# Another fixed order for the tasks of an attention stage

## The chip, the cores and the metric

The kernel runs on one core of a Trainium2 chip. The metric is the device time of one execution in microseconds (us), the median of three runs. The core's engines are named as in the profile: PE is TensorE (matmuls and transposes), PEld its loading of weights, DVE is VectorE, ACT is ScalarE, POOL is GpSimd and SP is SyncE, which here only starts DMA transfers.

## The reference

An attention over B = 4 batches, H = 8 heads, S = 576 positions and D = 64, with a second, linear "memory" branch, and behind it a mixture of 8 experts over all N = 2304 tokens, of which each token takes one:

```
scores = where(causal, -1e9, q @ k.T / sqrt(D))
a      = exp(scores - rowmax);  a /= a.sum(-1) + 1e-9
local  = a @ v
q_p    = elu(q) + 1
mem    = (q_p @ M_prev) / (q_p . z_prev + 1e-6)
x      = g * mem + (1 - g) * local          # g = sigmoid(beta) per head
# x as [2304, 512]
e      = argmax(x @ w_gate);  gate_w = softmax(x @ w_gate)[e]
eom    = sigmoid(x @ w_output_gate)[e]
out    = gate_w * eom * (relu(x @ w1[e]) @ w2[e])   # D = 512, F = 1024
```

All data are float32.

## The kernel before

**Tasks.** The attention, the routing and the first steps of the expert stage are cut into 1,181 small tasks. A task has a name, an engine and a function that issues a few instructions. The heads are taken two by two: a pair g (0 to 15) holds two heads of batch g // 4, and its 576 query positions are five tiles q (0 to 3 of 128 rows, 4 of 64). The names, with b for a batch:

- SSg_q: the scores of a query tile, on TensorE. One matmul is written as three with high and low parts (hi, lo). For q of 1 to 3 the two heads stand in the two halves of 64 rows of the array (L570); SSg_1 also holds q = 0. SSg_4 uses the full array (L557).
- Mg_q_j: mask and maximum on VectorE (L628, L596), from PSUM to the tile st. Eg_q_j: exponential and row sum on ScalarE. Tg_q_j: transposes of the probabilities on TensorE into a PSUM tile pt (L645, L614). Vg_q_j: the copy from pt to PT (L492).
- Pg_r_i: the product of probabilities and values, for query rows from r on (0 or 256; for the last pair 0, 128, ... 512). A matmul writes 64 columns of the array's output (L680). Og_r: its copy to oT (L492).
- Cg, Rg, F0g, F1g, F2g: the split of a pair's data into hi and lo, and phi, the elu + 1; F2 is on VectorE (L520).
- MEb_q: the memory product of a batch's query tile, 2 x 4 small matmuls over halves of 64 rows (L736), into two tiles me_0 and me_1. N1b_q and N2b_q normalise and scale it on VectorE (L742, L749), Gb_q sums logits (L752).
- PVb_q: transposes of oT on TensorE (L799); Wb the weights 1 / sum (L767, L768) and Yb_q the weighting on VectorE (L803); XD and OUT add and store.
- LTb_i: local logits, four matmuls side by side of 32 columns each (L828), LC their copy, LS their transposes, LY, LB, LA, RT, Tgate, Tpos, RK, GP, GS the routing. PLlq_h, YLlq_h, XLlq_h are what the last batch has for PV, Y and XD.
- Z...: first steps of the expert with the most tokens, called the star. The expert stage behind the attention starts with its product he (L1123).

**Modes.** Each task of TensorE has a mode, by the shape of its tile of the array: F (full array: SSg_4, transposes, PV, PL, RK, GP), R (row tiles: the other scores and ME), C (column tiles: P) and L (narrow column tiles: LT).

**What sets the order.** No scheduler decides: a string `ORDER` lists all tasks, and a loop issues them in that order. So the string sets the program order of every engine. Behind a colon stands the engine of a copy (tasks V, O, C and LC), ACT or DVE, since either can do it:

```
    def copy(e, dst, src):
        (A.copy if e == "ACT" else V.tensor_copy)(dst(), src())
...
    by = {t.name: t for t in jobs}
    for item in ORDER:
        name, _, eng = item.partition(":")
        by[name].fn(eng)
```

Engines run on their own and wait for each other by semaphores. Every TensorE task writes PSUM tiles from pools that give out free buffers: tag s (scores) has 4 buffers, tag pt (transposed probabilities) 2, and tag m has 2, for everything else: P, ME (which takes both), PV, LT, LS, RK, GP. A task waits until the readers of a buffer's former tile are done.

Of the kernel before, what the change touches and what calls it, by code (L numbers as in the profile page):

```python
# [55 lines left out]
C3:DVE F12 P1_0_0 E2_1_0 V1_4_1:DVE T2_0 load4 E1_3_0 E1_3_1 V2_0:DVE SS2_2 R3 M2_2_0 M2_2_1 O0_256:ACT O1_0:ACT SS2_3 T2_1 T1_3_1 load_v3 E2_2_0
V2_1:ACT M2_3_0 V1_3_1:ACT TS1_0 E2_3_0 SS2_4 T1_3_0 V1_3_0:ACT M2_3_1 MW1 F13 F04 E2_2_1 T2_2_0 T2_3_0 TS1_1 ranks M2_4_0 P1_256_0 C4:DVE E2_3_1 F22 MC1
V2_2_0:ACT SS3_1 M3_0_0 V2_3_0:ACT P1_256_1 T2_2_1 M3_1_0 M2_4_1 E2_4 V2_2_1:ACT E3_0_0 load5 F23 O1_256:DVE M3_0_1 T2_3_1 TS2_0 load6 E3_0_1 E3_1_0
V2_3_1:DVE SS3_2 ME0_0 M3_2_1 T2_4 E3_2_1 R4 M3_1_1 wgz V2_4_0:ACT N10_0 N20_0 V2_4_1:ACT F06 SS3_4 T3_2_1 T3_0 M3_2_0 ME0_1 F14 V3_0:ACT M3_4_0
V3_2_1:ACT SS4_1 M3_4_1 E3_2_0 N10_1 SS4_2 E3_1_1 N20_1 T3_1 T3_2_0 C5:ACT P2_0_0 P2_256_0 TS2_1 E3_4 M4_0_0 V3_1:ACT M4_0_1 F24 M4_2_1 G0_1 M4_2_0  # L60
V3_2_0:ACT O2_0:ACT E4_0_1 E4_0_0 T3_4 M4_1_1 E4_1_1 E4_2_1 P2_256_1 V3_4_0:DVE TS3_0 M4_1_0 O2_256:DVE T4_0 SS3_3 E4_1_0 load_v4 E4_2_0 V3_4_1:DVE
M3_3_0 ME0_4 C6:ACT V4_0:ACT T4_2_0 SS4_4 V4_2_0:ACT R5 N10_4 T4_2_1 R6 TS3_1 N20_4 M3_3_1 M4_4_0 V4_2_1:ACT T4_1 E3_3_0 M4_4_1 load7 E3_3_1 V4_1:ACT
ME0_3 SS4_3 E4_4 T3_3_1 V3_3_1:ACT T3_3_0 N10_3 V3_3_0:ACT N20_3 M4_3_0 F16 E4_3_0 M4_3_1 ME0_2 N10_2 TS4_0 F05 SS5_1 SS5_2 N20_2 F26 T4_4 M5_0_0
M5_0_1 E4_3_1 P3_0_0 V4_4_0:DVE P3_256_0 O3_0:ACT E5_0_0 load9 P4_0_0 E5_0_1 M5_1_0 G0_3 P3_256_1 load_v5 F15 C7:ACT M5_2_0 W0 O3_256:ACT T4_3_0
O4_0:ACT F07 V4_4_1:DVE F25 E5_1_0 R7 T4_3_1 PV0_2 M5_2_1 M5_1_1 PV0_1 SS5_4 V4_3_1:ACT E5_1_1 E5_2_1 V4_3_0:DVE T5_0 Y0_2 G0_4 V5_0:ACT E5_2_0 Y0_1
M5_4_0 SS5_3 G0_0 M5_4_1 LT0_0 load8 XD0_1 LC0_0:DVE T5_2_0 V5_2_0:ACT XD0_2 M5_3_1 T5_1 PV0_4 E5_4 M5_3_0 T5_2_1 SS6_2 SS6_1 V5_2_1:DVE F09 V5_1:ACT
E5_3_0 E5_3_1 Y0_4 OUT0_2 M6_0_0 LT0_1 F08 M6_2_1 LC0_1:ACT T5_4 load_v7 OUT0_1 E6_0_0 V5_4_0:ACT F19 M6_2_0 LM2 LS0 SS6_4 TS5_1 V5_4_1:ACT TS5_0
E6_2_1 F17 M6_1_0 TS4_1 T5_3_1 T5_3_0 LY0 XD0_4 M6_0_1 E6_0_1 LB0 G0_2 V5_3_1:ACT V5_3_0:ACT PV0_0 P4_256_0 M6_1_1 T6_2_1 F18 LA0 RT0_0 Y0_0 E6_1_1
E6_1_0 RT0_1 T6_0 SS7_1 XD0_0 P4_256_1 P5_256_0 O4_256:ACT V6_0:ACT V6_2_1:DVE M6_4_0 RT0_2 E6_2_0 C8:ACT R8 F27 RT0_3 RT0_4 M7_0_0 P5_0_0 P5_256_1
OUT0_4 T6_1 CA0 F28 E7_0_0 O5_0:ACT M6_4_1 E6_4 O5_256:DVE T6_2_0 load_v6 V6_2_0:ACT M7_0_1 M7_1_1 ME1_0 SS6_3 M7_1_0 SS7_3 load_v8 V6_1:ACT load10  # L70
E7_1_1 RX0 N11_0 E7_0_1 C9:ACT T6_4 N21_0 V6_4_0:ACT E7_1_0 PV0_3 M6_3_1 E6_3_1 M6_3_0 P6_0_0 Y0_3 V6_4_1:DVE TS6_0 E6_3_0 T7_0 O6_0:DVE M7_3_0 M7_3_1
# [4 lines left out]
SS9_1 O6_256:ACT E8_3_1 F013 O7_0:DVE T8_2_1 T8_1 F210 V8_2_1:ACT F211 M9_0_0 M9_0_1 PV1_0 T8_2_0 E8_3_0 V8_1:ACT P7_256_0 Tgate40 M9_1_1 W1 E9_0_1
V8_2_0:ACT Y1_0 M9_1_0 XD1_0 P7_256_1 load12 E9_0_0 T8_3_0 O7_256:ACT G1_4 G1_3 E9_1_1 V8_3_0:ACT PV1_1 OUT1_0 E9_1_0 F113 CJ0 LM3 load_v9 PV1_2
T8_3_1 Y1_1 Y1_2 SS8_4 M8_4_0 T9_0 M8_4_1 PV1_3 LT1_0 C11:ACT V8_3_1:ACT XD1_1 SS9_3 SS9_2 E8_4 V9_0:ACT G1_2 Y1_3 OUT1_1 M9_3_1 M9_3_0 load_v10 R11
LT1_1 XD1_2 T9_1 V9_1:ACT E9_3_0 SS9_4 LC1_0:DVE LC1_1:DVE LS1 TS8_0 XD1_3 M9_2_1 T8_4 E9_3_1 M9_2_0 LY1 V8_4_0:ACT SS10_1 LB1 OUT1_3 RK0 Tpos10
V8_4_1:ACT OUT1_2 T9_3_1 E9_2_1 PV1_4 LA1 M10_0_0 T9_3_0 Y1_4 RT1_0 V9_3_1:ACT M10_0_1 T9_2_1 E9_2_0 RT1_1 Tpos20 M9_4_0 V9_2_1:ACT C12:ACT P8_256_0  # L80
P8_0_0 Tpos30 M10_1_1 M10_1_0 P8_256_1 Tpos40 M9_4_1 RT1_2 CB0 F213 E10_0_1 V9_3_0:ACT T9_2_0 E10_0_0 E10_1_0 V9_2_0:ACT O8_0:DVE T10_0 E9_4 RT1_3
E10_1_1 V10_0:ACT O8_256:DVE RT1_4 SS10_2 M10_2_1 M10_2_0 E10_2_1 SS10_3 TS9_1 ME2_0 M10_3_0 R12 N12_0 load_v11 RX1 T10_1 SS10_4 SEL0_3 V10_1:ACT
E10_3_0 SEL0_2 ZI T9_4 N22_0 V9_4_0:ACT G2_0 TS9_0 E10_2_0 ME2_3 M10_3_1 SS11_1 C13:ACT V9_4_1:DVE E10_3_1 N12_3 R13 XD1_4 T10_2_1 T10_3_0 N22_3
V10_3_0:DVE M10_4_0 M11_0_0 E11_0_0 V10_2_1:ACT P9_256_0 P9_0_0 P9_256_1 M11_1_0 O9_0:ACT TS8_1 G2_3 T10_2_0 load15 O9_256:ACT T10_3_1 OUT1_4 F015
M10_4_1 V10_2_0:ACT M11_0_1 V10_3_1:ACT M11_1_1 Tgate11 Tgate31 E11_1_0 E10_4 E11_0_1 E11_1_1 SEL0_1 ME2_1 N12_1 SS11_3 N22_1 SS11_4 T10_4 RK1
V10_4_0:ACT MW3 T11_0 M11_4_0 Tpos11 M11_3_0 load14 TS10_1 V10_4_1:ACT V11_0:ACT MC3 T11_1 M11_3_1 V11_1:ACT ME2_4 Tpos21 CA1 CJ1 CB1 SS11_2 M11_4_1
E11_4 SS12_1 E11_3_1 N12_4 N22_4 T11_4 ZC M11_2_1 E11_3_0 TS11_1 M11_2_0 Z1 Z2 Tpos31 load_v12 M12_0_0 Z3 Z4 G2_1 V11_4_0:DVE Z5 P11_0_0 TS11_0
O11_0:ACT P10_256_0 P10_0_0 P10_256_1 F115 Tpos41 Z6 Z7 E12_0_0 Tgate21 M12_0_1 Z8 Z9 Z10 V11_4_1:DVE O10_0:ACT O10_256:DVE TS10_0 T11_3_0 T11_3_1
V11_3_1:DVE E11_2_1 M12_1_0 M12_1_1 ZN ME2_2 E12_0_1 C14:ACT N12_2 V11_3_0:ACT Tgate41 N22_2 E11_2_0 SS12_3 W2 T11_2_1 V11_2_1:ACT T11_2_0 SEL1_3
SS12_4 E12_1_0 PV2_1 T12_0 load_v14 V11_2_0:ACT E12_1_1 V12_0:ACT M12_3_1 M12_3_0 F215 P11_256_0 G2_2 SEL1_4 M12_4_0 Y2_1 E12_3_1 E12_3_0 SS13_1  # L90
P11_256_1 M12_4_1 SEL1_2 T12_1 M13_0_0 T12_3_1 M13_1_0 O11_256:ACT M13_0_1 V12_1:ACT M13_1_1 E12_4 XD2_1 PV2_4 PV2_3 R14 Y2_4 E13_1_1 T12_3_0 E13_0_1
SS12_2 SS13_3 XD2_4 OUT2_1 OUT2_4 V12_3_1:ACT V12_3_0:DVE M12_2_1 G2_4 E13_1_0 GA1 E13_0_0 T12_4 Y2_3 V12_4_0:ACT E12_2_1 F014 LT2_0 M12_2_0 LT2_1
T13_0 F012 SEL1_1 XD2_3 V12_4_1:DVE T13_1 LC2_0:DVE LC2_1:ACT V13_0:DVE M13_3_0 LS2 E12_2_0 V13_1:ACT SS13_2 T12_2_0 T12_2_1 E13_3_0 V12_2_1:ACT LY2
P12_0_0 M13_3_1 TS12_0 SEL0_4 load_v13 V12_2_0:ACT M13_2_0 O12_0:ACT PV2_0 LB2 M13_2_1 E13_2_0 SS13_4 T13_3_0 PV2_2 Y2_0 F112 F114 T13_2_0 Y2_2
V13_2_0:DVE XD2_0 Tgate50 Tgate51 OUT2_3 M13_4_0 E13_2_1 E13_3_1 F212 V13_3_0:ACT F214 P12_256_0 P13_0_0 P12_256_1 C15:DVE R15 O13_0:ACT SS14_1
# [1708 lines left out]
```

## Time and profile before

| what | value |
|---|---|
| median of 3 runs | 468.71 us (468.43 to 469.22) |
| profiled execution | 468.34 us |
| its span, first to last instruction | 466.3 us |
| TensorE busy | 456.7 us, 98% |
| VectorE busy | 284.9 us, 61% |
| ScalarE busy | 262.4 us, 56% |
| GpSimd busy | 271.1 us, 58% |
| granted TensorE clock, mean over the span | 0.996 of full speed |
| attention, up to the start of the expert stage's product he | 201.81 us |

Shares are means over the whole span. Busy time of TensorE counts from a matmul's start to its modelled end, and matmuls overlap, so it is an upper bound; starts are exact. The profiled execution is one; its time lies 0.37 us below the median.

### The profile page before, as it was taken

Reading aid. Unit: us, or ns where it says so; the run is one execution under the profiler, and the core shown is the slowest. Engines: PE = TensorE matmul, PEld = TensorE weight load, DVE = VectorE, ACT = ScalarE, POOL = GpSimd, SP = SyncE. Lnnn points to the kernel's source line nnn. Section 1 sums busy time; section 2 is a strip of 40 time slices with the busy share of each in tenths; the row PEclk is TensorE's granted clock in tenths of the full one; section 3 lists DMA queues with packets and bytes.
Section 4 is the critical chain, followed back from the end, with each engine's and each line's share of the span. In section 5 each row is a group of like instructions: output and inputs, shape, how many; then the busy total and the mean of one; then the engine's idle time right before and its main releaser. Section 6 shows DMA issues by size and latency. Waiting matters only on the chain.

```text
span 466.3 us, 10798 instructions
## 1 busy us (share of the span) xinstructions
PE 456.7 (98%) x3517; PEld 354.8 (76%) x3517; DVE 284.9 (61%) x851; ACT 262.4 (56%) x625; POOL 271.1 (58%) x274
## 2 busy tenths in 40 slices
...
GB/s 239 204 144 143 21 216 158 158 58 199 30 153 30 86 181 99 59 142 153 47 265 324 299 309 170 328 46 346 265 202 341 115 208 221 124 147 182 29 31 39
DMA packets 30119, 75.90 MB, mean 163 GB/s; under 512 B 4307, under 2 KB 4839, under 8 KB 30058
## 3 DMA queue, kind: packets, MB, share of 16 engines
...
q14 instruction: 28, 0.23, 0.1%
...
## 4 chain that ended last, share of the span: by engine, by line
PE 88%; DVE 3%; issue 2%; POOL 2%; ACT 2%; DVEq 1%; POOLq 0%; ACTq 0%
PE py L1432 18%; PE h L1432 17%; PE po L680 10%; PE pt L645 8%; PE s L570 7%; PE me L736 4%; PE hp L1458 3%; PE cy L1601 3%; PE ch L1601 3%; PE sd L557 3%; PE pt L614 2%; PE px L1400 2%; PE he L1123 1%; PE pv L799 1%; PE pl L904 1%
## 5 line engine op out<-in xcount | busy, mean ns | idle before, releaser
L633 ACT ACTIVATE st<-st,nm 128x128 f32<-128x128 f32 (+3 forms) x128 | 71.4, 562 | 3.7 <-DVE nm L628 3.6
L1465 POOL TENSOR_TENSOR hl<-hT,hh 128x512 fp32r<-128x512 f32 x32 | 43.5, 1380 | 40.6 <-ACT hh L1464 40.5
L628 DVE CUSTOM_DVE_ANT_0 st<-s,mask 128x128 f32<-128x128 f32 (+3 forms) x128 | 58.2, 483 | 8.2 <-PE s L570 4.1
L1108 DVE CAST whi<-kept 128x1024 fp32r<-128x1024 f32 x32 | 26.0, 811 | 51.6 <-ACTq L1439 40.7
L465 POOL TENSOR_TENSOR lo<-qk,hi 128x1216 fp32r<-128x1216 f32 x15 | 42.1, 2805 | 24.7 <-ACT hi L461 19.5
L1111 DVE TENSOR_TENSOR wlo<-kept,whi 128x1024 fp32r<-128x1024 f32 x32 | 54.4, 1701 | 1.1
L492 ACT COPY PT<-pt 128x512 f32<-128x512 f32 (+2 forms) x89 | 45.2, 523 | 15.9 <-PE pt L645 13.8
L1432 PE MATMUL h<-whi,xh 128*128 (+1 forms) x136 | 53.9, 396 | 0.0
L1432 PE MATMUL h<-whi,xl 128*128 (+1 forms) x136 | 53.4, 393 | 0.0
L1432 PE MATMUL h<-wlo,xh 128*128 (+1 forms) x136 | 53.4, 392 | 0.0
L1432 PE MATMUL py<-whi,hh 128*128 (+1 forms) x128 | 51.9, 406 | 0.0
L1432 PE MATMUL py<-whi,hl 128*128 (+1 forms) x128 | 50.2, 392 | 0.3 <-POOL hl L1465 0.3
L1432 PE MATMUL py<-wlo,hh 128*128 (+1 forms) x128 | 50.2, 392 | 0.0
L680 PE MATMUL po<-PT,v 128*64 128x320 f32 (+4 forms) x480 | 49.1, 349 | 0.8 <-ACT oT_hT L492 0.4
L645 PE MATMUL pt<-ident,st 128*128 128x128 f32 x320 | 48.0, 280 | 0.4 <-ACT st L633 0.4
L1464 ACT CAST hh<-hp 128x512 fp32r<-128x512 f32 x32 | 19.1, 598 | 50.6 <-PE py L1432 50.6
L1445 ACT ACTIVATE h<-h 128x1024 f32<-128x1024 f32 x17 | 17.5, 1029 | 47.9 <-PE h L1432 47.9
L680 PEld LDWEIGHTS po<-PT,v 128*64 128x64 f32 x480 | 29.6, 137 | 17.7 <-issue 2.8
L1411 POOL TENSOR_TENSOR xl<-x,xh 128x512 fp32r<-128x512 f32 x16 | 21.7, 1358 | 34.3 <-issue 19.0
L645 PEld LDWEIGHTS pt<-ident,st 128*128 128x128 f32 x320 | 35.2, 142 | 7.8 <-ACT st L633 2.5
...
L1432 PEld LDWEIGHTS h<-whi,xh 128*128 128x128 f32 x136 | 25.5, 188 | 6.0 <-ACT h L1445 0.3
...
## 6 DMA issues: line engine op xcount, KB each, us to landing
...
```

What stands on the lines that cost most here:

```text
L465: G.tensor_tensor(c["lo"][:, TQ:], c["raw"][:, TQ:], f32(c["hi"])[:, TQ:], op=ALU.subtract)
L492: (A.copy if e == "ACT" else V.tensor_copy)(dst(), src())
L570: T.matmul(c()["ss", q][j], l[r, lc], m[r, KC:KC + w], start=(a == 0), stop=(a == 2))
L628: V.tensor_tensor_reduce(st[:, :w], c()["ss", qt][j], mask[:, 512 - w:512], -SCALE, 3.0e38, ALU.add, ALU.min, negm()[:, i:i + 1])
L633: A.activation(st, st, AF.Exp, bias=c()["negm"][:, i:i + 1], scale=-1.0, accum_out=sums()[:, qt, 2 * p + j:2 * p + j + 1])
L645: T.transpose(pt[:, (m * k1 + i) * P:(m * k1 + i + 1) * P], st[:, i * P:(i + 1) * P], ident)
L680: T.matmul(po[64 * j:64 * j + 64, qs - q0:q1 - q0], vt[:, k, 64 * j:64 * j + 64], PT[:, j, k, qs:q1], start=(k == 0), stop=(k == kn - 1))
L1108: join((A.copy if eng is A else eng.tensor_copy)(whi[:, e % 2, c, :], raws[e, c]))
L1111: join(eng.tensor_tensor(wlo[:, e % 2, c, :], raws.pop((e, c)), f32(whi[:, e % 2, c, :]), op=ALU.subtract))
L1432: i = T.matmul(o[n % nh], l[:, z], m[:, n * 512 + part.start:n * 512 + part.stop], start=(c == 0 and k == 0 and n < nh), stop=(c == 3 and ...
L1465: G.tensor_tensor(hl[:, z], hT[:, z], f32(hh)[:, z], op=ALU.subtract)
L1601: i = apart(T.matmul(o[w * q:w * q + w], x[:, z:z + w], wide[b][:, m + size * q:m + size * q + size], start=(j == 0), stop=(j == len(todo) ...
```

## The change

Only the string `ORDER` is another. It holds the same tasks; 55 of its lines differ. No function, no tile and no buffer count changes. Two of the lines, the first from before and the second from the change, in the stretch of batch 1:

```
--- before.py
+++ after.py
...
-R9 TS6_1 V7_0:ACT SS7_2 ME1_4 N11_4 E7_3_0 T6_3_1 T7_1 E7_3_1 SS7_4 V7_1:ACT N21_4 M7_2_0 Tgate10 E7_2_0 V6_3_1:ACT M7_2_1 ME1_2 G1_0 N11_2 SS8_1
...
+ME1_4 RX0 SS8_1 C9:ACT M6_3_0 TS6_0 N11_4 SS7_2 R9 N21_4 V7_0:DVE M7_2_0 V7_1:ACT E7_2_0 ME1_2 T7_3_0 M7_2_1 N11_2 T6_3_1 N21_2 E6_3_0 TS6_1 Tgate10
...
```

TensorE's 295 tasks of the attention stand in 118 changes of mode before and in 108 after. Of the copies, 61 change engine: 34 go from ScalarE to VectorE and 27 from VectorE to ScalarE. ScalarE has 129 copies after 136, VectorE 55 after 48.

**TensorE, around two memory products of batch 1.** The rows of before, from ME1_4 to ME1_2 (a row is one or more equal instructions, `out<-inputs`, with the tile's name and number; pt is a tile of transposes, sd the scores SS7_4). The first two rows are the last of ME1_4, the last row the first of ME1_2:

```order
L736 MATMUL me1_4_0_1500<-mz1_491,phi7_1085 128x81
L736 MATMUL me1_4_1_1501<-mz1_491,phi7_1085 128x81
L645 MATMUL pt6_3_1_1515<-ident_77,st6_3_1_1466 128x128 x4
L645 MATMUL pt7_1_0_1520<-ident_77,st7_1_0_1424 128x128 x2
L645 MATMUL pt7_1_0_1520<-ident_77,st7_1_1_1402 128x128 x2
L557 MATMUL sd7_4_0_1526<-lo7_1069,hi7_1068 128x288
L557 MATMUL sd7_4_0_1526<-hi7_1068,lo7_1069 128x288
L557 MATMUL sd7_4_0_1526<-hi7_1068 128x288
L557 MATMUL sd7_4_1_1530<-lo7_1069,hi7_1068 128x288
L557 MATMUL sd7_4_1_1530<-hi7_1068,lo7_1069 128x288
L557 MATMUL sd7_4_1_1530<-hi7_1068 128x288
L736 MATMUL me1_2_0_1547<-mz1_491,phi4_588 128x81
```

Six transposes of T6_3_1 and T7_1 and the full-array scores of pair 7 stood between the two products. The same place in the change; the first two rows are the last of SS8_1, of which 12 rows follow directly behind ME1_4:

```order
L570 MATMUL s8_1_0_1499<-hi8_1340 128x128
L570 MATMUL s8_1_1_1500<-hi8_1340 128x128
L570 MATMUL s7_2_0_1523<-lo7_1068,hi7_1067 128x384
L570 MATMUL s7_2_1_1524<-lo7_1068,hi7_1067 128x384
L570 MATMUL s7_2_0_1523<-hi7_1067,lo7_1068 128x384
L570 MATMUL s7_2_1_1524<-hi7_1067,lo7_1068 128x384
L570 MATMUL s7_2_0_1523<-hi7_1067 128x384
L570 MATMUL s7_2_1_1524<-hi7_1067 128x384
L736 MATMUL me1_2_0_1540<-mz1_500,phi4_576 128x81
L736 MATMUL me1_2_1_1541<-mz1_500,phi4_576 128x81
```

T6_3_1, T7_1 and SS7_4 have moved behind ME1_2; between the two products stand SS8_1 and SS7_2, which like ME are in mode R.

**VectorE, ahead of y1_0.** Y1_0 frees the PSUM buffer of PV1_0. The rows of before, from the phi of pair 10 on (nm is the tile of maxima; the one-element rows belong to them):

```order
L520 SCALAR_TENSOR_TENSOR phi10_1703<-qk10_1437,phi10_1703 128x576
L520 SCALAR_TENSOR_TENSOR phi11_1683<-qk11_1617,phi11_1683 128x576
L628 ISA st9_0_0_1780,nm9_1781<-s9_1_0_1749,mask_138 128x128
L628 ISA nm9_1781 128x1
L628 ISA st9_0_1_1783,nm9_1781<-s9_1_1_1750,mask_138 128x128
L628 ISA nm9_1781 128x1
L298 TENSOR_SCALAR gw0_1541<-gw0_1541 128x5
L628 ISA st9_1_1_1802,nm9_1781<-s9_1_1_1750,mask_138 128x256
L628 ISA nm9_1781 128x1
L767 SCALAR_TENSOR_TENSOR rr1_1804<-sums1_833,gc_89 128x40
L768 RECIPROCAL rr1_1804<-rr1_1804 128x40
L803 TENSOR_TENSOR y1_0_1809<-pv1_0_1785,rr1_1804 128x512
```

Three maxima of pair 9 and no copy stood ahead of it. The same place in the change:

```order
L520 SCALAR_TENSOR_TENSOR phi10_1711<-qk10_1478,phi10_1711 128x576
L520 SCALAR_TENSOR_TENSOR phi11_1674<-qk11_1634,phi11_1674 128x576
L628 ISA st8_2_1_1777,nm8_1578<-s8_2_1_1627,mask_138 128x384
L628 ISA nm8_1578 128x1
L298 TENSOR_SCALAR gw0_1572<-gw0_1572 128x5
L492 COPY PT0_127<-pt8_1_0_1747 128x2x2x128
L628 ISA st8_2_0_1797,nm8_1578<-s8_2_0_1626,mask_138 128x384
L628 ISA nm8_1578 128x1
L767 SCALAR_TENSOR_TENSOR rr1_1799<-sums1_823,gc_89 128x40
L768 RECIPROCAL rr1_1799<-rr1_1799 128x40
L752 TENSOR_REDUCE lg1_1397<-x1_3_1690 128x16
L803 TENSOR_TENSOR y1_0_1808<-pv1_0_1786,rr1_1799 128x512
```

Two maxima of pair 8 over 384 columns, a copy of 512 columns (V8_1) and a sum of logits (G1_3) now stand ahead of y1_0; the maxima of pair 9 have moved behind it.

## Rows read from the trace of the kernel before

**Rows 1.** The page, part 1: busy time, share of span, instructions.

```profile
PE 456.7 (98%) x3517; PEld 354.8 (76%) x3517; DVE 284.9 (61%) x851; ACT 262.4 (56%) x625; POOL 271.1 (58%) x274
```

**Rows 2.** Stretches: length; busy PE, PEld, DVE, ACT, POOL; clock; DMA share; GB/s.

```profile
80.00:100.00 20.00, 20.00 (x208) 16.20 (x205) 18.63 (x69) 17.92 (x49) 12.36 (x11) 1.00 0.32 120
```

**Rows 3.** TensorE's waits, by place: total, number, mean in us.

```profile
PE warm L192 <- DVE ones L940: 1.1, 1, 1.1
PE po L680 <- ACT oT_hT L492: 0.4, 1, 0.4
```

**Rows 4.** Timeline of TensorE, 60 to 75: start, length in us, instruction, operands.

```profile
61.67 0.38 PE L645 MATMUL pt<-ident,st 128*128 128x128 f32 x2
61.98 0.51 PE L570 MATMUL s<-lo,hi 64*128 64x512 f32 x2
62.31 0.40 PE L570 MATMUL s<-hi,lo 64*128 64x512 f32 x2
62.55 0.41 PE L570 MATMUL s<-hi 64*128 64x512 f32 x2
62.88 0.69 PE L828 MATMUL lt<-oT,wgz 128*32 128x288 f32 x8
63.51 0.98 PE L645 MATMUL pt<-ident,st 128*128 128x128 f32 x7
64.33 0.60 PE L799 MATMUL pv<-ident,oT 128*64 128x128 f32 x4
...
69.12 1.03 PE L645 MATMUL pt<-ident,st 128*128 128x128 f32 x8
69.99 0.60 PE L799 MATMUL pv<-ident,oT 128*128 128x128 f32 x4
```

**Rows 5.** Timeline of TensorE, 81 to 89.

```profile
81.66 0.87 PE L680 MATMUL po<-PT,v 128*64 128x256 f32 x8
82.46 0.44 PE L645 MATMUL pt<-ident,st 128*128 128x128 f32 x2
82.83 0.44 PE L570 MATMUL s<-lo,hi 64*128 64x384 f32 x2
...
83.46 1.01 PE L736 MATMUL me<-mz,phi 64*128 64x81 f32 x16
84.40 1.09 PE L645 MATMUL pt<-ident,st 128*128 128x128 f32 x8
...
86.21 1.12 PE L736 MATMUL me<-mz,phi 64*128 64x81 f32 x16
87.13 0.37 PE L570 MATMUL s<-lo,hi 64*128 64x256 f32 x2
...
87.95 1.09 PE L645 MATMUL pt<-ident,st 128*128 128x128 f32 x8
```

**Rows 6.** The chain that ended last: start, length in us, what.

```profile
96.19 2.85 PE po L680 x28
...
101.56 2.21 PE po L680 x20
...
201.81 2.58 PE he L1123 x6
```

**Rows 7.** Timeline of VectorE, near 87 and from 95 to 103.

```profile
87.37 0.23 DVE L742 SCALAR_TENSOR_TENSOR nr<-me,gt 128x4 f32<-128x4 f32 x2
...
87.87 0.89 DVE L749 TENSOR_TENSOR x<-me,nr 128x320 f32<-128x320 f32 x2
...
95.58 0.55 DVE L628 CUSTOM_DVE_ANT_0 st<-s,mask 128x384 f32<-128x384 f32 x1
...
98.46 1.42 DVE L520 SCALAR_TENSOR_TENSOR phi<-qk,phi 128x576 f32<-128x576 f32 x2
...
102.09 0.69 DVE L803 TENSOR_TENSOR y<-pv,rr 128x512 f32<-128x512 f32 x1
```

**Rows 8.** Groups by line and shape: copies; count, busy us, mean ns, idle before.

```profile
L492 ACT COPY PT<-pt 128x512 f32<-128x512 f32 x51 | 29.2, 580 | 10.9 <-PE pt L645 9.1 <-PE pt L614 1.5
...
L492 DVE COPY PT<-pt 128x512 f32<-128x512 f32 x13 | 9.0, 689 | 2.1 <-PE pt L614 1.0 <-PE pt L645 1.0
```

More of the change, by code (lines that the diff above doesn't have):

```diff
@@ L56 @@
[L56 to L71, printed above, removed]
@@ L76 @@
[L76 to L91, printed above, removed]
@@ L92 @@
[L92 to L95, printed above, removed]
@@ L100 @@
-V14_4_0:DVE TS15_0 E15_1_1 G3_1 W3_0 V14_4_1:ACT TS15_1 O14_0:DVE O13_256:ACT E15_0_1 TS14_1 T15_4 PLl4_0 M14_2_1 PLl1_0 V15_4_0:ACT fetch3 YLl4_0
-TL4_0 E14_2_1 YLl1_0 T15_0 XLl4_0 PLl0_0 YLl0_0 V15_4_1:ACT V15_0:ACT XLl1_0 TS14_0 SS15_3 M14_2_0 ME3_3 Tgate60 TL1_0 E15_1_0 M15_3_0 N13_3 E14_2_0
-load_v15 T15_1 N23_3 T14_2_1 SS15_2 W3_1_4 V15_1:ACT M15_2_0 T14_2_0 E15_3_0 V14_2_0:ACT PLl2_0 ZX YLl2_0 ZY XLl0_0 V14_2_1:ACT W3_1_0 M15_3_1 M15_2_1
-P15_512_0 fetch4 P15_0_0 TL2_0 G3_0 O15_512:ACT O15_0:ACT P15_128_0 P14_256_0 E15_2_0 O15_128:DVE E15_2_1 P14_256_1 TL0_0 W3_1_1 W3_1_2 PLl1_1 LA2
@@ L104 @@
-E15_3_1 W3_1_3 O14_256:ACT YLl1_1 XLl2_0 PLl4_1 PLl3_0 YLl4_1 GP0 T15_3_0 TL1_1 V15_3_0:ACT XLl1_1 XLl4_1 TL4_1 YLl3_0 PLl0_1 T15_3_1 GS0 RT2_0 GO0
-RT2_1 RT2_2 RT2_3 GP1 T15_2_0 YLl0_1 RT2_4 Tgate12 GS1 V15_3_1:ACT OL4 RX2 GO1 RK2 V15_2_0:ACT CA2 Tpos12 Tgate32 Tpos22 Tgate22 CJ2 T15_2_1 Tpos32
-Tgate42 V15_2_1:ACT GA2 CB2 Tgate52 P15_384_0 O15_384:ACT P15_256_0 Tpos42 Tgate62 TL0_1 TL3_0 XLl3_0 XLl0_1 PLl3_1 G3_3 SEL2_0 OL1 O15_256:ACT SEL2_3
-SEL2_2 SEL2_4 G3_2 SEL2_1 PLl2_1 YLl3_1 YLl2_1 XLl3_1 XLl2_1 GP2 GS2 OL0 OL2 OL3 GO2 TL2_1 TL3_1
+T0_2_1 M1_1_0 V0_2_0:ACT F20 E0_4 V0_2_1:DVE M1_1_1 load3 C2:ACT fill0 M1_0_1 E1_0_0 load_v2 R2 P0_0_0 E1_1_1 load_v1 T0_4 F02 E1_1_0 fill17
```

63 lines of the change are left out of this document (53 added, 10 removed).

## The prediction, made blind

> **What bounds the kernel now.** I read the page's shares first, then the stretches, the waits, and last the order of starts on TensorE. TensorE is busy 98% of the span [rows 1]. The change lies in the attention, the first 202 us; the expert stage behind it is not touched. In the stretch 80 to 100 TensorE is busy all the time, VectorE 18.63 us of 20 and ScalarE 17.92 [rows 2]. So TensorE looks like the bound, with VectorE close behind. The view of TensorE's waits shows little: behind the first one of all (1.1 us, at the very start) the longest is 0.4 us [rows 3]. A busy share can hide waits, because a record of a matmul is longer than the distance to the next start, so I looked at the starts themselves. They are evenly spaced: eight transposes from 69.12 to 69.99 us are 0.109 us apart [rows 4]. Almost nothing waits in the middle of the attention; TensorE issues as fast as its own work lets it. Only work taken from TensorE, or waits added to it, can move the end.
>
> [...]
>
> **What a change of mode costs.** Tasks stand in four modes: full array (F), row tiles (R: scores of 64 rows and the memory products), column tiles (C: PV products of 64 columns) and narrow column tiles (L, the LT tasks). A visit to row tiles, from [rows 4]:
> - the way in: two transposes and the step to the scores take 61.67 to 61.98, 0.31 us, against 2 x 0.109 = 0.22 inside a mode: 0.09;
> - the first pair of the scores takes 61.98 to 62.31, 0.33 us, the next of the same size 62.31 to 62.55, 0.24: 0.09;
> - the way out: the last pair of that size takes 62.55 to 62.88, again 0.33 against 0.24: 0.09;
> - the transposes after a change: seven take 63.51 to 64.33, 0.82 us, against 7 x 0.109 = 0.76: 0.06.
>
> That is 0.33 us for a visit, two changes, or 0.165 each. A visit to column tiles: the eight matmuls of PV block 6 that stand alone take 81.66 to 82.46, 0.80 us [rows 5]. In a run the same eight cost the difference between 28 and 20 matmuls, 2.85 - 2.21 = 0.64 us [rows 6], so 0.16 more alone. With the way in of 0.09 and the transposes after it (0.06) a visit is 0.31 us, again some 0.16 a change.
>
> [...]
>
> **The change, part by part.** I counted modes through both orders, over 295 TensorE tasks. Before there are 118 changes, after 108. F to R goes from 30 to 23, R to F 30 to 27, C to F 20 to 18, L to F 4 to 3, R to C 3 to 2; C to R rises by 1, F to L by 1, L to R by 2; the others stay. Net 10 fewer, at 0.16: **-1.6 us** of TensorE's work. [...] The work itself is the same: every task is in both orders, the expert stage's text is the same, and no DMA is added.
>
> Copies that change engine: 61, of which 34 go to VectorE and 27 to ScalarE. VectorE has 18 of the 512-wide ones after 13, at 0.689 us against 0.580 on ScalarE [rows 8]. With each size at its own row's mean VectorE gets some 4.4 us more and ScalarE 3.8 less. I cost it at nothing on average: VectorE has 1.4 us free in a full stretch of 20 [rows 2], which makes some 14 over the attention. Where that cover is gone it comes back as a wait, so I looked at what a shifted order brings close together.
>
> First place, the memory products of batch 1. Each takes both buffers of tag m, and VectorE frees them by normalising and scaling: from 87.37 to 88.7, some 1.35 us, starting 0.24 us after the product's successor starts at 87.13 [rows 5, 7]. With a semaphore's delay the next product can start some 1.7 us after. Before, 1.81 us of full-array work stood in between (84.40 to 86.21) [rows 5]. After, only SS8_1 and SS7_2 do: 0.82 (87.13 to 87.95) and 0.63 (82.83 to 83.46), 1.45 us [rows 5]. A wait of 0.3 us, or 0.9 if VectorE does M6_3_0 first, which the order puts ahead; I take 0.4.
>
> Second place, the PV transposes of batch 1. PV1_1 needs a buffer that VectorE's y1_0 frees. Ahead of y1_0 from phi10 on stand two phi (1.42 us), two maxima over 384 (0.55 each), a copy of 512 (0.69), the weights, a sum and y1_0 itself (0.69): 3.9 us of those with a row and some 4.9 in all, where before it took 4.2 with an idle piece in it (98.46 to 102.7) [rows 7, 8]. TensorE has only T8_3_0, PV1_2 and T8_2_0 between PV1_0 and PV1_1, some 1.2 us, where two PV pieces (2.21 us) [rows 6] stood before. I take a wait of 0.4 us, bounds 0 and 1.0.
>
> At the end of the attention O15_128 now stands on ScalarE behind two exponentials of block 2, and PLl1_1 waits for it; in turn T15_2_0 and T15_2_1 find theirs done long before, and P15_384 no longer waits for gs1. I put this at zero, within 0.5 either way.
>
> Waits that go: in the order before, P10_256_0 stood behind a buffer that the star's first step frees, and SS12_1 behind the maxima of batch 2; both have more work ahead now. Neither can be over the longest of [rows 3], 0.4 us; I take 0.6 for both together.
>
> Sum: -1.6 + 0.4 + 0.4 - 0.6 = **-1.4 us**. The profiled execution took 468.34 us, 466.3 of span and 2.0 around it, so it would take 466.9; it lies 0.4 under the median of the three runs, 468.71, which would come to **467.3 us**.
>
> The attention's end passes its shift on: the expert stage's matmuls (he, from 201.81 us) follow it directly in the chain that ended last [rows 6], and the transfers of the star's weights are issued in the same places of the text.
>
> **The rivals.** About 0.2%, 0.94 us, is what a measurement can tell from no change.
> 1. *The forecast*: -0.95 to -2.4 us, 467.3. Chance 0.50.
> 2. *No gain*: the changes go, but VectorE sets the pace and hands the time back. The two places at their upper ends (0.9 + 1.0) less 1.6 is +0.3, so 469.0; if TensorE never was the bound, 468.7. For it: VectorE at 93% of the stretch of [rows 2]. Against: the even starts. Chance 0.28.
> 3. *Slower*: VectorE late at the end of each batch. There the norms, y and sums of a whole batch meet the copies that are new on VectorE; at the second place 4.9 us of its work meet about 3.9 us of TensorE's, 1.0 us. At three batch ends that is 3.0; with no old wait gone the sum is -1.6 + 3.0 = +1.4, 470.1 us. It decides from 2.5 us of new waits on. For it: 4.4 us of added work. Against: batch ends where copies went the other way. Chance 0.16.
> 4. *More*: the price at its upper bound (2.1) and 1.0 us of old waits gone with no new ones: -3.1, 465.6. Chance 0.06.
>
> **How the numbers follow.** Faster by over 0.2%: all of 4 and of 1, 0.56. Within: 2, 0.28. Slower: 3, 0.16. The predicted time is the first case's. A range from 465.6 to 469.8 leaves out some of 3 and little else; the likeliest case's own is 466.3 to 467.8.
>
> **What would show it.** TensorE's start of the expert stage (he, now at 201.81) should come 1.4 us sooner, with T15_2_1 ahead of po15_384 and no wait there. The shift should grow in small steps along the attention, not at one place. Waits at me1_2 and pv1_1 of 0.3 to 0.5 us, with VectorE as releaser, would show the two places right; over 1 us, rival 3. If the starts after a change are as costly but the end does not move, rival 2. [...]

## The result and the profile after

The changed kernel takes 475.45 us (median of 4 runs, 474.81 to 475.87) against 468.79 for the kernel before: 1.4% slower, ratio 1.0141, 95% interval 1.0129 to 1.0153. Forecast were 467.3 us and a range up to 469.8. The profiled execution took 475.87 us with a span of 474.2.

The page, part 1, answers to [rows 1]:

```profile
PE 459.5 (97%) x3517; PEld 355.1 (75%) x3517; DVE 291.8 (62%) x858; ACT 258.9 (55%) x618; POOL 269.8 (57%) x274
```

VectorE is busy 6.9 us longer over the span. Up to the start of he it is 183.0 us after 172.0, so 11.0 us more, and the copies bring only 4.3 of these. The stretches, columns as in [rows 2]:

```profile
60.00:80.00 20.00, 18.78 (x171) 13.72 (x169) 18.14 (x54) 15.48 (x44) 12.21 (x11) 1.00 0.50 164
80.00:100.00 20.00, 19.13 (x197) 15.56 (x195) 18.84 (x65) 15.09 (x42) 10.05 (x7) 1.00 0.42 130
```

TensorE is no longer busy all the time, and VectorE does fewer instructions (65 in place of 69 in the second stretch) in more time. The granted clock is 1.00 in both stretches, as before. TensorE's waits between 20 and 200 us, which were two or three of at most 0.4 us [rows 3]; the five largest of ten:

```profile
PE pt L645 <- ACT PT L492: 0.9, 3, 0.4
PE pv L799 <- DVE y L803: 0.8, 1, 0.8
PE s L570 <- DVE nm L628: 0.6, 1, 0.6
PE pt L645 <- ACT st L633: 0.5, 1, 0.5
PE pt L645 <- DVE PT L492: 0.4, 1, 0.4
```

And the first product of the expert stage in the chain that ended last, at 201.81 before [rows 6]:

```profile
208.50 2.58 PE he L1123 x6
```

So 6.7 us are lost by the end of the attention. Busy records hide a part of TensorE's waits, so I counted them from its starts: for each step between two starts I took the shortest of its kind in either trace; where the second task starts within 0.34 us of the end of what it waits for, the rest of the step is a wait. That sums to 4.0 us before and 12.0 after. The waits grew by 8.1 us and the end moved by 6.7 to 6.8, so about 1.3 us of work did go. The sums hang on what counts as one kind of step: with finer and coarser kinds the added waits come to between 4.5 and 8 us and the work that went to between 0.4 and 1.6, so the 1.3 us are an estimate and not shown.

The cause shows in the groups by line and shape. The group of phi (L520) stands first of before (in the first fence) and then of the change (in the second), where the weights (L767) and the copies that answer to [rows 8] are added:

```profile
L520 DVE SCALAR_TENSOR_TENSOR phi<-qk,phi 128x576 f32<-128x576 f32 x16 | 12.2, 772 | 0.0
```

```profile
L520 DVE SCALAR_TENSOR_TENSOR phi<-qk,phi 128x576 f32<-128x576 f32 x16 | 16.0, 1007 | 1.5 <-ACT phi L517 1.5
...
L492 DVE COPY PT<-pt 128x512 f32<-128x512 f32 x18 | 12.3, 682 | 1.7 <-PE pt L614 1.2 <-PE pt L645 0.4
...
L767 DVE SCALAR_TENSOR_TENSOR rr<-sums,gc 128x40 f32<-128x40 f32 x3 | 2.7, 903 | 0.0
```

The copies last what they lasted. But the same 16 phi take 3.8 us more, and an instruction over 40 columns 0.9 us on average. The timeline of VectorE in the change shows three long ones behind which TensorE waited:

```profile
45.19 1.84 DVE L520 SCALAR_TENSOR_TENSOR phi<-qk,phi 128x576 f32<-128x576 f32 x1
46.95 0.48 DVE L492 COPY oT<-po 128x320 f32<-128x320 f32 x1
...
61.16 2.33 DVE L767 SCALAR_TENSOR_TENSOR rr<-sums,gc 128x40 f32<-128x40 f32 x1
63.53 0.40 DVE L768 RECIPROCAL rr<-rr 128x40 f32<-128x40 f32 x1
64.03 0.69 DVE L803 TENSOR_TENSOR y<-pv,rr 128x512 f32<-128x512 f32 x1
...
79.74 3.14 DVE L520 SCALAR_TENSOR_TENSOR phi<-qk,phi 128x576 f32<-128x576 f32 x1
82.81 0.18 DVE L267 TENSOR_REDUCE mx<-wt 128x5 f32<-128x40 f32 x1
```

They are F24, W0 and F27. GpSimd's timeline in the same stretches, tasks R, which subtract hi to make lo (L465):

```profile
43.59 2.82 POOL L465 TENSOR_TENSOR lo<-qk,hi 128x1216 fp32r<-128x1216 f32 x1
...
60.65 2.78 POOL L465 TENSOR_TENSOR lo<-qk,hi 128x1216 fp32r<-128x1216 f32 x1 [2.06 <-ACT hi L461]
...
79.45 2.82 POOL L465 TENSOR_TENSOR lo<-qk,hi 128x1216 fp32r<-128x1216 f32 x1 [2.28 <-ACT hi L461]
```

Each of the three starts inside a subtraction and ends just behind it: 47.03 after 46.41, 63.49 after 63.43, 82.88 after 82.27. All three read two tensors from SBUF, as the subtraction does. Below, "held" means this. The next instruction of VectorE started within 0.1 us of the held one's end (46.95, 63.53 and 82.81), so all behind it is late by 1.1, 2.1 and 2.4 us, and TensorE's largest waits follow: T4_2_0 and T4_2_1 (0.9 us together, for copies), PV0_2 and SS5_3 (2.1 us), SS6_3 and SS7_3 (1.6 us). A fourth long hold, Tgate11 (1.85 us in place of 0.19 at 133.86, also inside a subtraction), is followed by no wait of TensorE, so it cost nothing. The last pair of waits on TensorE:

```profile
83.22 0.99 PE L570 MATMUL s<-lo,hi 64*128 64x512 f32 x2
83.72 0.73 PE L570 MATMUL s<-hi,lo 64*128 64x512 f32 x2
84.06 0.62 PE L570 MATMUL s<-hi 64*128 64x512 f32 x2
85.28 0.83 PE L570 MATMUL s<-lo,hi 64*128 64x512 f32 x2 [0.60 <-DVE nm L628]
```

In the kernel before the subtraction of the same pair 8 ran from 77.00, and the rows that VectorE did during it have their usual length; each reads at most one tensor from SBUF, the other operand is PSUM, and nm is one value a row (GpSimd's row in the first fence, VectorE's in the second):

```profile
77.00 2.83 POOL L465 TENSOR_TENSOR lo<-qk,hi 128x1216 fp32r<-128x1216 f32 x1 [2.58 <-ACT hi L461]
```

```profile
76.40 0.75 DVE L520 SCALAR_TENSOR_TENSOR phi<-qk,phi 128x576 f32<-128x576 f32 x1
77.07 0.51 DVE L596 CUSTOM_DVE_ANT_0 st<-sd,maskd,nm 128x288 f32<-128x288 f32 x1
77.50 0.49 DVE L492 COPY oT_h<-po 128x320 f32<-128x320 f32 x1
```

The phi at 76.40 is F28. It began 0.6 us ahead of the subtraction, and nothing was held: it took 0.75 us, the subtraction 2.83. In the traces of before and of the change, five VectorE instructions of two SBUF tensors began inside a subtraction over 0.02 us ahead of its end, the three above, Tgate10 and Tgate11, and each ended 0.06 to 0.62 us behind it. The phi at 95.13 in the change began 0.02 us ahead of the end of one and took 0.74 us. With one operand in PSUM nothing was held: in the change x<-me,nr (L749), at 93.47 and 93.88, took 0.49 and 0.48 us as outside a subtraction, and Tgate10 behind it, at 94.28 in the same subtraction (92.36 to 95.15), 0.93 in place of 0.19. The same shows at GpSimd's additions XD (L807, 1.28 us), which also read two tensors: in the change F212 and CJ0 were held behind them for 0.6 and 0.7 us (1.31 in place of 0.75, 0.87 in place of 0.15). The prediction had not weighed it.

### The profile page after: what moved, and what is told of

Same layout as the page of the kernel before. It is cut to its first block, busy times and chain, and to the rows that moved or that the text cites. A ratio compares the mean times of both kernels' runs of the same rounds, so it can differ in the third digit from the quotient of the medians.

```text
span 474.2 us, 10816 instructions
## 1 busy us (share of the span) xinstructions
PE 459.5 (97%) x3517; PEld 355.1 (75%) x3517; DVE 291.8 (62%) x858; ACT 258.9 (55%) x618; POOL 269.8 (57%) x274
## 4 chain that ended last, share of the span: by engine, by line
PE 56%; DVE 3%; POOL 2%; issue 2%; DMA 1%; ACT 0%; POOLq 0%; DVEq 0%; ACTq 0%
PE h L1432 19%; PE py L1432 18%; PE hp L1458 3%; PE cy L1601 3%; PE ch L1601 3%; PE px L1400 2%; PE pye L1140 1%; PE he L1123 1%; PE me L736 1%; DMA out<-ye,rowe 1%; PE pl L904 1%; PE po L680 1%; PE pt L645 1%; PE chp L1615 0%; DVE st L628 0%
## 5 line engine op out<-in xcount | busy, mean ns | idle before, releaser
L633 ACT ACTIVATE st<-st,nm 128x256 f32<-128x256 f32 (+3 forms) x128 | 71.2, 558 | 12.4 <-DVE nm L628 12.4
L1465 POOL TENSOR_TENSOR hl<-hT,hh 128x512 fp32r<-128x512 f32 x32 | 47.1, 1491 | 46.0 <-ACT hh L1464 41.8
L1108 DVE CAST whi<-kept 128x1024 fp32r<-128x1024 f32 x32 | 29.8, 930 | 57.5 <-ACTq L1439 42.7
L465 POOL TENSOR_TENSOR lo<-qk,hi 128x1216 fp32r<-128x1216 f32 x15 | 41.9, 2796 | 24.3 <-ACT hi L461 18.0
L492 ACT COPY PT<-pt 128x512 f32<-128x512 f32 (+2 forms) x80 | 39.9, 521 | 16.3 <-PE pt L645 13.7
L1111 DVE TENSOR_TENSOR wlo<-kept,whi 128x1024 fp32r<-128x1024 f32 x32 | 46.5, 1455 | 1.1
L1432 PEld LDWEIGHTS h<-whi,xl 128*128 128x128 f32 x136 | 25.5, 188 | 5.9 <-DVE xl L1411 0.2
```

The lines of the kernel that those rows point to most:

```text
L465: G.tensor_tensor(c["lo"][:, TQ:], c["raw"][:, TQ:], f32(c["hi"])[:, TQ:], op=ALU.subtract)
L633: A.activation(st, st, AF.Exp, bias=c()["negm"][:, i:i + 1], scale=-1.0, accum_out=sums()[:, qt, 2 * p + j:2 * p + j + 1])
L1108: join((A.copy if eng is A else eng.tensor_copy)(whi[:, e % 2, c, :], raws[e, c]))
L1111: join(eng.tensor_tensor(wlo[:, e % 2, c, :], raws.pop((e, c)), f32(whi[:, e % 2, c, :]), op=ALU.subtract))
L1432: i = T.matmul(o[n % nh], l[:, z], m[:, n * 512 + part.start:n * 512 + part.stop], start=(c == 0 and k == 0 and n < nh), stop=(c == 3 and ...
L1465: G.tensor_tensor(hl[:, z], hT[:, z], f32(hh)[:, z], op=ALU.subtract)
```

## The experiments

Theories: **A**, VectorE is held behind GpSimd; **B**, the copies that went to VectorE make it late; **C**, two tight places as forecast; **D**, the order is too tight whatever holds VectorE. Times of before beside each are those of the same comparison. Of lines of `ORDER` only the pieces that matter are shown.

**Three held tasks moved** in the changed kernel:

```diff
-P2_0_0 F24 E4_0_1
+P2_0_0 E4_0_1
...
-V3_4_1:DVE load_v4
+V3_4_1:DVE F24 load_v4
...
-E5_1_0 O3_0:DVE
+E5_1_0 W0 O3_0:DVE
...
-M5_0_1 V4_4_1:ACT G0_4 W0
+M5_0_1 V4_4_1:ACT G0_4
...
-RT0_0 T6_0 RT0_1 M6_4_0
+RT0_0 T6_0 RT0_1 F27 M6_4_0
...
-R8 F27 RT0_3
+R8 RT0_3
```

> Theory A (VectorE held by GpSimd): in the changed kernel three VectorE instructions with two SBUF inputs start while GpSimd subtracts hi from data (lo) and last 1.84, 2.33 and 3.14 us in place of 0.75, 0.19 and 0.75, 5.6 us in all; TensorE's start of he came 6.7 us late. This kernel is the changed one with three tasks moved so that they run outside those spans: F24 behind V3_4_1, W0 ahead of O3_0, F27 behind RT0_1. By A some 4 to 5.5 us come back: 470 to 471.5 us, and the three instructions last 0.75, 0.2 and 0.75. Theory B (the copies that went to VectorE make it late): nothing that matters changes, 474.5 to 475.5. Theory C (two tight places, ME1_2 and PV1_1, as forecast): no change, 475.

472.52 us against 469.11, ratio 1.0061 (1.0042 to 1.008): 2.9 us back by three moves on VectorE alone, less than A's 4 to 5.5. In the profiled execution the three have their usual lengths, but F25 now met an addition of GpSimd's (1.30 us), and the third hold passed on to the next instruction of two SBUF inputs, RT0_4 (VectorE's timeline, then GpSimd's):

```profile
79.77 2.36 DVE L270 SCALAR_TENSOR_TENSOR oha<-mx,wt 128x40 bf16<-128x40 f32 x1
```

```profile
79.25 2.82 POOL L465 TENSOR_TENSOR lo<-qk,hi 128x1216 fp32r<-128x1216 f32 x1 [2.27 <-ACT hi L461]
```

This execution was the slowest of the five (474.38). TensorE's granted clock was 0.50 in it from 14.37 to 17.78 us, ahead of all that was moved (0.992 over the whole execution); it lost 2.0 us against the change up to SS1_3 and gained 3.1 behind it.

**One hold put into the kernel before:**

```diff
-CA0 F28 E7_0_0
+CA0 E7_0_0
...
-O5_256:DVE T6_2_0
+O5_256:DVE F28 T6_2_0
```

> The kernel before with one task moved: F28 (phi of pair 8, needed only a batch later) from behind CA0 to behind O5_256, two VectorE instructions later, so that it starts after GpSimd's lo of pair 8 instead of 0.6 us ahead of it. Theory A: it lasts some 2.5 to 3.2 us in place of 0.75, VectorE is 2 us late near 80 us, TensorE waits there, 469.7 to 471 us. Theories B and C: no change, 468.5 to 469.

470.68 us against 469.11, ratio 1.0031 (1.0019 to 1.0042), 1.6 us slower. F28 on VectorE, the subtraction on GpSimd, and the wait of TensorE (at SS7_3):

```profile
78.84 2.78 DVE L520 SCALAR_TENSOR_TENSOR phi<-qk,phi 128x576 f32<-128x576 f32 x1
```

```profile
78.20 2.80 POOL L465 TENSOR_TENSOR lo<-qk,hi 128x1216 fp32r<-128x1216 f32 x1 [2.59 <-ACT hi L461]
```

```profile
PE s L570 <- DVE nm L628: 1.1, 1, 1.1
```

One task two places later costs 1.6 us, by A alone: no copy and no order on TensorE is touched. (In the trace the product he starts 3.0 us later, but 1.2 of these are there at SS6_3 already, ahead of the move; this execution was the slowest of seven.)

**Order and engines crossed.** Only the letters behind the colons change; a line of each, the changed order with the engines of before, and the order of before with those of the change:

```diff
-V0_4_0:ACT M1_2_0 SS1_4 E1_0_1 T1_0 M1_2_1 V0_4_1:ACT
+V0_4_0:DVE M1_2_0 SS1_4 E1_0_1 T1_0 M1_2_1 V0_4_1:ACT
...
-SS1_4 fill17 V0_4_0:DVE M1_2_1 V0_4_1:ACT T1_0
+SS1_4 fill17 V0_4_0:ACT M1_2_1 V0_4_1:ACT T1_0
```

> The changed order with every copy on the engine that it had before. Theory B: VectorE gets 4.4 us less, the waits for maxima and copies go, 470 us or less. Theory A: the three held instructions stand where they stood, so most of the loss stays: 473 to 476, unless their starts shift against GpSimd's.

> The order of before with every copy on the engine that it has in the change. Theory B: slower, 472 us or more. Theory A: within 1.5 us of before (467.5 to 470), unless a two-input instruction of VectorE now falls behind a subtraction on GpSimd, which would show as one that lasts 1 to 3 us.

477.97 us (1.0184, 1.0166 to 1.0202) and 483.28 (1.0308, 1.0283 to 1.0333). B is refuted as it stood: giving VectorE its 4.4 us back makes the changed order 2.5 us slower. But A's numbers were wrong too. In the first, none of the three holds is left; F28 is held for 1.8 us, and most of TensorE's waits are for copies, on both engines. So the first tests A as little as it bears out B. In the second, 14 us came in place of under 1.5. It seems that the engines suit only the order for which they were set. In the second a single hold is the largest wait (VectorE, then TensorE's wait for a copy queued behind it):

```profile
44.59 3.23 DVE L520 SCALAR_TENSOR_TENSOR phi<-qk,phi 128x576 f32<-128x576 f32 x1
```

```profile
PE pte L616 <- DVE PT L492: 3.0, 1, 3.0
```

TensorE was busy 1.0 of the 4 us up to 50, and from 50.25 to 53.66 its granted clock was 0.50; half of these 3.41 us, some 1.7, is an estimate of what the clock added to the loss.

**More tasks moved away**, on top of the first kernel:

```diff
-R8 RT0_3 RT0_4 M6_4_1
+R8 RT0_3 M6_4_1
...
-T6_1 CA0 F28 SS7_1
+T6_1 SS7_1
...
-M7_1_1 V6_2_0:ACT
+M7_1_1 RT0_4 CA0 F28 V6_2_0:ACT
```

and F25 behind M5_4_1; Tgate10, F29, Tgate30 behind MC2; CJ0 behind G1_3; F214 behind G2_2.

> The changed order with all VectorE instructions of two SBUF inputs that were held over 0.5 us before 170 us moved out of GpSimd's two-input spans, bar the one near 133 us behind which nothing waited: the three of the first try, and RT0_4, CA0 and F28 (in the first try the hold of 2.4 us had passed on to RT0_4's instruction), F25, Tgate10, F29, Tgate30, CJ0 and F214. Theory A: the waits for maxima at SS7_3 (0.8 us) and SS5_3 (0.5), those at ME1_1 (0.5), SS9_3 with LT1_1 (0.8) and ME3_1 (0.35) go, 2 to 3 us under the first try: 469 to 471. If the rest of its loss over before is not from holds (theory D: the order is too tight for VectorE and ScalarE whatever holds them), 472 to 473.

473.4 us against 468.62 (1.0093, 1.0077 to 1.011), no better. The waits at SS5_3, ME1_1, SS9_3 and LT1_1 went as expected, but all times had shifted, the subtraction began 2.2 us sooner, and RT0_2 was now held (VectorE, then TensorE's waits):

```profile
77.27 2.61 DVE L264 SCALAR_TENSOR_TENSOR wt<-dl,edesc 128x40 f32<-128x40 f32 x1
```

```profile
PE pt L645 <- DVE PT L492: 1.5, 1, 1.5
PE pv L799 <- DVE x L749: 0.5, 1, 0.5
```

**RT0_1 to RT0_3 moved too, behind M7_1_1**; and on top of it **E3_0_1 behind V2_4_1**:

```diff
-E3_2_1 E3_0_1 V2_4_0:ACT V2_4_1:ACT
+E3_2_1 V2_4_0:ACT V2_4_1:ACT E3_0_1
```

> The second try with RT0_1, RT0_2 and RT0_3 moved as well, to the place of RT0_4 behind M7_1_1. In the second try GpSimd's lo of pair 8 began 2.5 us sooner, RT0_2's instruction fell behind it and lasted 2.6 us, and the copy V6_0 behind it kept T6_2_0 waiting for 1.6 us. Theory A: no VectorE instruction lasts over 1 us too long between 40 and 130 us, T6_2_0 does not wait, and 1.5 to 2.2 us come back: 471.0 to 472.0. Theory D (the order is too tight for VectorE whatever holds it): another wait takes the place of this one, 472.5 or more.

> The kernel of e8_routing_later with one exponential, E3_0_1, moved from ahead of the two copies V2_4_0 and V2_4_1 on ScalarE to behind them. In the change T3_2_1 waits 0.6 us for these copies. If an exponential of 128 columns (0.59 us with its read of the sum) in front of a copy is the cause of that wait, 0.4 to 0.6 us come back against e8_routing_later; if ScalarE is late there anyway, nothing.

472.23 (1.0084, 1.0063 to 1.0104) and 472.08 (1.0078, 1.0061 to 1.0094). In the first, T6_2_0 waits no more, but the moved routing made PV0_3 wait (1.1 us in the view of waits). In the second, the wait of T3_2_1 fell from 0.61 to 0.22 us, but the product he started only 0.2 us sooner (205.42 after 205.61): the next waits took the rest, as D has it for this place. The 0.15 us between the two times are less than either interval.

**Those side effects mended** (RT0_0 to RT0_4 and F27 right behind LA0, CA0 and F28 behind M6_4_1, Tgate10, F29, Tgate30 behind M8_0_0):

```diff
-F18 LA0 M6_1_0
+F18 LA0 RT0_0 RT0_1 RT0_2 RT0_3 RT0_4 F27 M6_1_0
...
-ME1_1 M8_0_0 SS8_2
+ME1_1 M8_0_0 Tgate10 F29 Tgate30 SS8_2
```

> The kernel of e8_routing_later with its own side effects mended: there the routing instructions behind M7_1_1 made N1 of the memory product ME1_0 late, so that PV0_3 waited 1.3 us, and Tgate10, F29 and Tgate30 made SS8_2 wait 0.9 us. Now RT0_0 to RT0_4 and F27 stand right behind LA0, ahead of the lo of pair 8, CA0 and F28 behind M6_4_1, the three others behind M8_0_0. Theory A: 1.3 to 2.2 us back against e8_routing_later, 470.0 to 471.0; with that 4.5 to 5.5 of the 6.7 us are holds. Theory D: other waits take their place, 472.

475.02 us (1.0125, 1.0097 to 1.0154), a miss. At 93 us TensorE was 1.5 us ahead of the kernel that this one builds on; then F29 fell 0.03 us behind the subtraction of pair 10 (VectorE, GpSimd, TensorE's wait at ME1_3):

```profile
92.92 3.35 DVE L520 SCALAR_TENSOR_TENSOR phi<-qk,phi 128x576 f32<-128x576 f32 x1
```

```profile
92.89 2.77 POOL L465 TENSOR_TENSOR lo<-qk,hi 128x1216 fp32r<-128x1216 f32 x1
```

```profile
PE me L736 <- DVE x L749: 2.4, 1, 2.4
```

The wait is not all that it lost. TensorE was busy 1.6 of the 4 us up to 98, and from 97.50 to 104.33 its granted clock was 0.50. The page shows it in the ninth of 40 slices of 11.8 us, in tenths of full speed:

```profile
PEclk9999999979999999999999999999999999999998
```

Its lag behind the kernel it builds on grew in that time from 0.04 us (ME1_3) to 3.44 (P7_0_0) and stayed there. This holds for the profiled execution, 475.52 us; the other three took 474.48 to 476.80.

**The subtraction in four pieces**, in the changed kernel and in the kernel before:

```diff
-        G.tensor_tensor(c["lo"][:, TQ:], c["raw"][:, TQ:], f32(c["hi"])[:, TQ:], op=ALU.subtract)
+        [G.tensor_tensor(c["lo"][:, z], c["raw"][:, z], f32(c["hi"])[:, z], op=ALU.subtract) for z in (slice(TQ + 304 * i, TQ + 304 * i + 304) for i in range(4))]
```

> The changed kernel with its order untouched; GpSimd's subtraction that makes lo (1216 columns, 2.8 us) is issued in four pieces of 304 columns. If a VectorE instruction is held only until the GpSimd instruction that it meets has ended, no hold lasts over some 0.8 us and 3 to 5 us come back, less what four starts on GpSimd cost: 470.5 to 473. If it is held until GpSimd's queue is empty, or if the holds were not the cause, 475 to 476.

> The kernel before with the same split. It has no hold by a lo subtraction, so theory A expects no gain: 468.5 to 469.5, the upper end if the longer GpSimd work makes a score wait.

473.07 us (1.0082, 1.0065 to 1.0099), 2.4 us back with no task moved, less than the 3 to 5 expected, and 468.93 against 469.17 (0.9989, 0.9975 to 1.0003), no difference. In the changed kernel with the split, VectorE at the third place (it lost 2.4 us there before), then GpSimd:

```profile
78.77 1.17 DVE L520 SCALAR_TENSOR_TENSOR phi<-qk,phi 128x576 f32<-128x576 f32 x1
...
80.08 0.61 DVE L270 SCALAR_TENSOR_TENSOR oha<-mx,wt 128x40 bf16<-128x40 f32 x1
...
81.18 0.86 DVE L520 SCALAR_TENSOR_TENSOR phi<-qk,phi 128x576 f32<-128x576 f32 x1
```

```profile
78.48 4.27 POOL L465 TENSOR_TENSOR lo<-qk,hi 128x304 fp32r<-128x304 f32 x4 [2.28 <-ACT hi L461]
```

VectorE gets in between the pieces; now three instructions lose 0.4, 0.4 and 0.1 us, and GpSimd's four pieces take 4.27 us there. At 60.63, where W0 alone met them (0.37 us in place of 0.19), they take 3.22 us, against 2.78 in one piece. With the times shifted, F25 met an addition of GpSimd's, which was not split: it lasted 1.81 us at 63.91, and SS5_3 behind it waited as long as in the change.

**F29 out of the way**, and the same **with the split**:

```diff
-M8_0_0 Tgate10 F29 Tgate30 SS8_2
+M8_0_0 SS8_2
...
-ME1_3 Tgate20 F011
+ME1_3 F011
...
-N21_3 OUT0_3
+N21_3 Tgate10 F29 Tgate30 Tgate20 OUT0_3
```

> The kernel of e10_places with its one remaining long hold taken away: there F29 (phi of pair 9) began 0.03 us behind GpSimd's lo of pair 10 and lasted 3.35 us, and ME1_3 waited 2.5 us. Tgate10, F29, Tgate30 and Tgate20 now stand behind N21_3. Up to T6_3_0 that kernel was 1.0 us ahead of e8_routing_later and lost 5.0 us right behind it. Theory A: 469.5 to 471.0, which is 4.5 to 6 us of the change's loss given back by moves of VectorE tasks alone. Theory D: 472 or more, by waits that no hold explains.

> The kernel of e13_phi9_later with GpSimd's lo subtraction in four pieces. If e13_phi9_later has no hold left, no gain: the same or up to 0.5 us more. If it has one that the moves did not foresee, this one is 1 us or more faster.

470.86 us (1.0063, 1.0029 to 1.0098) and 470.0 (1.0023, 1.0013 to 1.0033) against 468.9. Of the first's nine runs seven took 469.87 to 471.68, the two others 474.04 and 476.67 (the last with a mean granted clock of 0.987); all ten of the second stayed within 469.24 to 471.35. The four largest of TensorE's waits in the first between 20 and 200 us, and its start of the expert stage:

```profile
PE pt L645 <- ACT PT L492: 0.6, 2, 0.4
PE pt L645 <- ACT st L633: 0.5, 1, 0.5
PE pl L904 <- ACT oT_hT L492: 0.4, 1, 0.4
PE pt L645 <- DVE PT L492: 0.3, 1, 0.3
```

```profile
203.72 2.58 PE he L1123 x6
```

So by the medians 4.6 us of the loss went by moving VectorE tasks alone, 5.5 with the split (the two intervals overlap); TensorE's order and the copies' engines are those of the change throughout.

**The price of a change of mode.** In the kernel before, nine transpose tasks moved behind the row-tile task that followed them; two of the nine:

```diff
-T3_2_1 T3_0 M3_2_0 ME0_1 F14 V3_0:ACT
+T3_2_1 M3_2_0 ME0_1 T3_0 F14 V3_0:ACT
...
-T5_2_1 SS6_2 SS6_1
+SS6_2 T5_2_1 SS6_1
```

> The kernel before with nine transpose tasks (T3_0, T4_1, T5_2_1, T7_2_0, T9_4, T11_1, T12_3_0, T13_2_1, T14_3_0) moved behind the row-tile task that followed them, so that each visit to row tiles is cut in two: 136 changes of mode in place of 118, the same work. At the forecast's 0.16 us a change: +2.9 us. At 0.13, which the comparison of the two traces without their waits gives: +2.3. At 0.09, only the step in front of the new mode: +1.6. Waits that this brings would come on top and show as such in the trace.

472.46 us against 468.62 (1.0081, 1.0064 to 1.0097), 3.8 us more. That is 0.21 us for each of 18 changes. By the count of waits used above 0.9 us of them are new waits, and 2.9 us by 18 is 0.16 us each.

**The tail alone:**

```diff
-P15_512_0 fetch4 P15_0_0 TL2_0 G3_0 O15_512:ACT O15_0:ACT P15_128_0 P14_256_0
+W3_1_0 P15_0_0 V15_1:ACT M15_2_1 P15_512_0
+E15_3_1 fetch4 O15_0:DVE M15_2_0 M15_3_0 P14_256_0 O15_512:DVE P15_128_0
```

(a piece of it; all behind SS15_4 as in the change, all ahead as before).

> The order of before up to SS15_4, behind it the rest in the order and with the engines of the change (116 changes of mode). In the trace of the change TensorE makes up 1.2 us between SS15_4 and the start of the expert stage. If that is the order's own merit, 467.3 to 468.1 us; if it only made up waits that it had before, no change, 468.7 to 469.2.

468.41 us against 468.62 (0.9996, 0.9986 to 1.0006): no difference that can be measured, though he starts at 201.29 in its trace. No version beat the kernel before.

## Why the prediction was wrong

- **The step that failed** is the cost of VectorE's work: "With each size at its own row's mean ..." and "I cost it at nothing on average". It took an instruction's length as given wherever it stands. F24, W0 and F27 lasted 7.3 us in place of 1.7, and TensorE waited 4.6 us for what stood behind them. Smaller holds of CJ0 (0.7 us) and Tgate10 (0.7 us) stood ahead of the waits at SS9_3, LT1_1 and ME1_1, 1.3 us more, which went when those tasks were moved. That is 5.9 of 8.1 us of added waits; the two kernels with F29 out of the way, in which nothing is held for over 1.0 us up to 128 us, give 4.6 and 5.5 us back. The work of the copies was sized right, 4.3 us measured against 4.4. The order showed where each of these tasks stood; whether it met the subtraction was a matter of 0.03 to 1.6 us, which no view of the trace before could settle. But that VectorE's two-input instructions and GpSimd's subtraction come close could be seen there, and it should have been a rival with a large price.
- **The price of a change** was near: 0.16 us forecast, 0.16 measured with the counted waits taken off and 0.21 without. The ten changes gave about 1.3 us (8.1 of waits less 6.8 of shift), 0.4 to 1.6 by other counts; forecast 1.6. The forecast's upper price for them, 2.1 us, from which the lower end of its range is worked out, is shown by no run; the counts here gave 1.6 at most, and the 0.21 us a change of the moved transposes holds their waits.
- **ME1_2**: a wait of 0.4 us forecast, 0.30 counted. The delay of 0.11 us that the forecast put between VectorE's end and the product's start measures 0.05 to 0.15 us where TensorE waited for VectorE in these two traces. **PV1_1**: 0.4 forecast, none there; its VectorE queue was not late.
- **Old waits**: those of P10_256_0 and SS12_1 went, 0.45 us of the 0.6 forecast. New ones of the same size came for copies on ScalarE (T3_2_1 0.6, T13_2_0 0.4, T2_2_1 0.3) and at ME3_1 (0.3); they stay when the holds go. With the holds mended the order is still about 1 to 2 us slower; that these waits are the reason was not tried.
- **The tail**, put at zero within 0.5, made up 1.2 us of TensorE's shift in the trace of the change; alone it is worth nothing measurable.
- **Behind the attention** the span after the start of he grew by 1.2 us (474.2 - 208.5 against 466.3 - 201.8). One wait of 1.0 us for GpSimd's hl stands there in the change, 0.3 before; why was not tried.
- **The rivals**: rival 3 had the right engine and sign, with 3.0 us of new waits against 8.1 counted, and for another reason, added copies at the ends of batches. With these copies left where they are, moving tasks and splitting the subtraction gave most of the loss back; and of the held tasks behind which TensorE waited most, only W0 stands at the end of a batch. The even starts, which spoke for TensorE as the bound, were right for the order before and say nothing of another.
